# Regrouping the columns of wqkv: matmuls of 512, 512, 384 and 320 columns in place of four of 432

## The chip, the core and the metric

The kernel runs on one core of a Trainium2 chip. The core has a matmul engine (TensorE, called PE in the profile; its weight loads stand in a row of their own, PEld), three engines for elementwise work (VectorE = DVE, ScalarE = ACT, GpSimd = POOL), and a sync engine (SP) that here issues nearly all DMA transfers. The metric is the device time of one execution in microseconds (us), as the median of several runs. Before the change it is 1163.93 us (three runs, 1163.89 to 1163.94).

## The reference

The input x has 2048 rows of D = 576. After a layernorm without scale or shift, two branches run on the same rows and are added to x:

```python
xn = layernorm(x)
return x + A(xn, wqkv, wo) + B(xn, w1, b1, w2, b2)

# A: attention, 32 heads of 18 columns, each row looks at 8 rows: itself and every second row back
q, k, v = split(xn @ wqkv)              # wqkv: 576 x 1728
logits = (q . k[pos - 2*w], w = 0..7) * 18**-0.5     # masked where pos - 2*w < 0
o = softmax(logits) . v[pos - 2*w]
A = o @ wo                              # wo: 576 x 576
# B: feed-forward with a squared relu
B = relu(xn @ w1 + b1)**2 @ w2 + b2     # w1: 576 x 4608, w2: 4608 x 576
```

Everything is float32 in and out. The matmuls get that accuracy by splitting each factor into a high part, rounded to the matmul's own format (F32R), and the low rest; a product is then hi·hi + hi·lo + lo·hi.

## The kernel before

**Blocks.** The 2048 rows are handled in NB = 4 blocks of TB = 512 rows. In every block the feed-forward loop runs over NF = 36 slices of 128 hidden columns: `ffn1` makes one slice of the hidden layer (14 matmuls of 512 columns, line 476), `ffn2` multiplies it with w2 into five PSUM accumulators (14 matmuls of 512 columns, line 499) two slices later. The contraction of 576 is cut into NC = 5 chunks of 128; the fifth holds the last 64 rows twice, so that a high and a low part share one matmul. That is why a full product takes 14 matmuls and not 15.

**Attention.** The 32 heads are dealt into G = 4 groups of 8, CG = 144 columns each. For one group g of one block, `qkv` runs 4 row tiles j of 128 rows; `qkv_rows` issues 14 matmuls (`three`, line 356) in which the rows' transposed x is the stationary operand, loaded as 128 x 128 weights, and the group's columns of wqkv stream past. Those columns are the group's 144 of Q, 144 of K and 144 of V, so each of these matmuls is 432 wide. The result lies in one PSUM tile `wk`, of which there are three, shared with `ffn1`. `qkv_out` copies it out in three ACT instructions: Q into `qo[b]` at the group's own columns, K and V into the group's `kv` tiles. `qkv_close` writes K and V to scratch in DRAM and reads them back with the 14 rows ahead of each partition's rows. Then `attention(b, g)`, a generator, is worked off in pieces on DVE and ACT between the feed-forward steps; it reads its group's columns of `qo[b]` and in the end writes the attention output over them. `o_chunk` and `o_acc` multiply the finished rows with wo into the same five accumulators.

**Weights.** `load_wq(g)` loads the group's columns chunk by chunk (75 DMAs of 128 x 432 into the two `wqr` buffers, line 344), and `split` makes the high part on ACT (line 116) and the low part on DVE (line 118) in the tiles `wqh` and `wql`, of which there is one each, WQ = 448 columns wide. It is called three or four steps ahead of the group's matmuls.

**The order.** `step(n)` goes through the 144 slices of all blocks. The table `pre` says at which step loads and groups stand: in block 0 the groups 1, 2 and 3 start at steps 9, 15 and 20, in later blocks group 0 starts two steps ahead of the block and groups 1 to 3 at its steps 4, 11 and 18. A scheduler then orders the instructions of each engine from a simulation of its own, so the places shift by some instructions; on PE most groups stand as 56 matmuls in a row (4 row tiles x 14), and group 0 of blocks 1 to 3 as 42 and 14 with matmuls of the output product between them.

**The opening.** Block 0's group 0 is written out by hand in `open_rows` (its own order on PE, ACT, DVE and POOL is kept): x is normalized and transposed on PE (line 170), and the 56 matmuls of line 225 follow as their inputs become ready. `load_first` brings the weights for it into one tile `raw`; the high parts are made on ACT, three low parts on DVE and two on POOL (line 200). Two further pieces bear on line numbers below: lines 547 and 549 are the last two output halves, made with matmuls of 256 columns, and line 604 is a warm-up of the matmul engine.

Of the kernel before, what the change touches and what calls it, by code (L numbers as in the profile page):

```python
# [8 lines left out]
F32 = mybir.dt.float32  # L9
F32R = mybir.dt.float32r  # L10
BF16 = mybir.dt.bfloat16
AF = mybir.ActivationFunctionType
# [4 lines left out]
P = 128  # L17
S, D, F = 2048, 576, 4608
H, DH, W, DIL = 32, 18, 8, 2
TB = 512  # L20
NB = S // TB
NJ = TB // P
NC = 5
NF = F // P
G = 4
HG = H // G
CG = HG * DH
HALO = (W - 1) * DIL
# [6 lines left out]
SCALE = DH ** -0.5  # L35
LAG = 2
WARM = 6
WQ, KV = 448, 2688


@with_exitstack
def block_kernel(ctx: ExitStack, tc: tile.TileContext, x, xt, wqkv, wo, w1, b1, w2, b2, out):
    nc = tc.nc
    const = ctx.enter_context(tc.tile_pool(name="const", bufs=1))
    mt = ctx.enter_context(tc.tile_pool(name="mt", bufs=1))
    sb = ctx.enter_context(tc.tile_pool(name="sb", bufs=1))
# [39 lines left out]
    xb, xT, xr, xh, xl, qo, ob, wq = {}, {}, {}, {}, {}, {}, {}, {}  # L86
# [9 lines left out]

    def load_first():
        xb[0] = sb.tile([P, NJ, D], F32, name="xb", bufs=1)
        raw = sb.tile([P, NC, TB], F32, name="xr", bufs=1)[:, :, :3 * CG]
        hi = mt.tile([P, NC, WQ], F32R, name="wqh")[:, :, :3 * CG]  # L100
        lo = mt.tile([P, NC, WQ], F32R, name="wql")[:, :, :3 * CG]
        nc.sync.dma_start(xb[0][:, 0, :288], xv[0, :, 0, :288])
        nc.scalar.dma_start(xb[0][:, 0, 288:], xv[0, :, 0, 288:])
        nc.scalar.dma_start(raw[:, 0], wqkv[0, :, 0])
        nc.sync.dma_start(xb[0][:, 1], xv[0, :, 1])
        for c in range(1, NC):
            nc.sync.dma_start(raw[:, c], wqkv[0, :, c])
        for j in range(2, NJ):
            nc.sync.dma_start(xb[0][:, j], xv[0, :, j])
        for scr in (kscr[0], vscr[0]):  # L110
            nc.sync.dma_start(scr[:PAD], zero)
        return raw, hi, lo
# [16 lines left out]
    def open_x(b):  # L129
        xh[b] = mt.tile([P, NC, TB], F32R, name="xh", bufs=2)  # L130
        xl[b] = mt.tile([P, NC - 1, TB], F32R, name="xl", bufs=2)
# [15 lines left out]
    def row_scale(j):  # L147
        mean_var(0, j)
        rs = sb.tile([P, 1], F32, name="rs", bufs=NJ)
        inverse_std(rs, ln[0, j][:, 1:2])  # L150
        return rs
# [37 lines left out]
    def open_rows():  # L189
        xn = sb.tile([P, NJ, NC * P], F32, name="xt", bufs=1)  # L190
        open_x(0)
        y = open_y()
        raw, hi, lo = first_wq
        rs = {}

        def w_hi(c):
            nc.scalar.activation(hi[:, c], raw[:, c], AF.Copy)

        def w_lo(c, eng):
            eng.tensor_tensor(out=lo[:, c], in0=raw[:, c], in1=hi[:, c].bitcast(F32), op=ALU.subtract)  # L200

        def stats(j, *ks):
            for k in ks:
                bn_stats(0, j, k)

        def scale(j):
            rs[j] = row_scale(j)

        def turn_rows(j):
            turn(y[0 if j % 2 else 3], xn, j, range(NC - 1))  # L210
            turn(y[1 if j % 2 else 4], xn, j, (NC - 1,))

        def take_rows(j, only=None):
            take(y[0 if j % 2 else 3], j, range(NC - 1), only)
            take(y[1 if j % 2 else 4], j, (NC - 1,), only)

        def part(j, i):
            hi, lo = qw[0]
            a, c = divmod(i, 10)
            js = slice(j * P, (j + 1) * P)  # L220
            if (0, j) not in qp:
                qp[0, j] = pw.tile([P, TB], F32, name="wk")
                done[j] = 0
            done[j] += 1
            nc.tensor.matmul(qp[0, j][:, :3 * CG], (xl if a == 1 else xh)[0][:, c, js], (lo if a == 2 else hi)[:, c],  # L225
                             start=done[j] == 1, stop=done[j] == 3 * NC - 1)

        def parts(j, *which):
            for i in which:
                part(j, i)  # L230

        done = {}
        act, dve = nc.scalar, nc.vector
        warm_up(4, TB, xb[0][:, 0, :1])
        stats(0, 0, 1)
        scale(0)
        warm_up(1, TB // 2, rs[0])
        w_hi(0)
        stats(1, 0)
        normalize_rows(xn, 0, rs[0], False, pieces=((0, 2 * P), (2 * P, D)))  # L240
        turn(y[0], xn, 0, (0, 1))
        turn(y[1], xn, 0, (2, 3))
        turn(y[2], xn, 0, (4,))
        w_hi(1)
        stats(1, 1)
        scale(1)
        take(y[0], 0, (0, 1))
        take(y[1], 0, (2, 3))
        normalize_rows(xn, 1, rs[1], False)
        w_hi(2)  # L250
        w_hi(3)
        w_lo(0, dve)
        take(y[2], 0, (4,))
        w_lo(1, nc.gpsimd)
        w_hi(4)
        qkv_open(0, 0, (hi, lo))
        parts(0, 0, 1, 10, 11, 2, 12, 3)
        turn_rows(1)
        take_rows(1, act)
        stats(2, 0, 1)  # L260
        w_lo(2, nc.gpsimd)
        scale(2)
        take_rows(1, dve)
        parts(0, 13, 20, 4)
        parts(1, 0, 1, 2, 3, 20)
        parts(0, 21)
        parts(1, 21, 10, 11, 12, 13, 4)
        nm = minus_mean(2, rs[2])
        normalize_rows(xn, 2, rs[2], True, nm)
        w_lo(3, dve)  # L270
        w_lo(4, dve)
        parts(0, 22)
        parts(1, 22)
        turn_rows(2)
        stats(3, 0, 1)
        scale(3)
        parts(0, 23)
        parts(1, 23)
        parts(0, 24)
        parts(1, 24)  # L280
        take_rows(2)
        nm = minus_mean(3, rs[3])
        qkv_out(0, 0, 0)
        normalize_rows(xn, 3, rs[3], True, nm)
        qkv_out(0, 0, 1)
        parts(2, 0, 1, 2, 3, 20, 21, 22, 23, 10, 11)
        turn_rows(3)
        take_rows(3)
        split_w1(0)
        parts(2, 12, 13, 4, 24)  # L290
        qkv_out(0, 0, 2)
        parts(3, 0, 1, 2, 3, 20, 21, 22, 23, 10, 11, 12, 13, 4, 24)
        split_w1(1)
        last_act = qkv_out(0, 0, 3)
        ffn1(0)
        qkv_close(0, 0)
        return last_act
# [38 lines left out]
    def xsplit(b, c):  # L336
        return xh[b][:, c], xl[b][:, c] if c < NC - 1 else None

    def load_wq(g):
        hi = mt.tile([P, NC, WQ], F32R, name="wqh")[:, :, :3 * CG]  # L340
        lo = mt.tile([P, NC, WQ], F32R, name="wql")[:, :, :3 * CG]
        for c in range(NC):
            r = sb.tile([P, 3 * CG], F32, name="wqr", bufs=2)
            nc.sync.dma_start(r, wqkv[g, :, c])
            split(hi[:, c], lo[:, c], r)
        wq[g] = hi, lo

# [2 lines left out]
    def three(ps, a_hi, a_lo, b_hi, b_lo):  # L350
        mm = []
        for c in range(NC - 1):
            mm += [(a_hi(c), b_hi(c)), (a_hi(c), b_lo(c)), (a_lo(c), b_hi(c))]
        mm += [(a_hi(NC - 1), b_hi(NC - 1)), (a_hi(NC - 1), b_lo(NC - 1))]
        for i, (l, r) in enumerate(mm):
            nc.tensor.matmul(ps, l, r, start=i == 0, stop=i == len(mm) - 1)  # L356

    qw, qp = {}, {}
# [8 lines left out]
    def qkv_rows(b, g, j):  # L367
        hi, lo = qw[g]
        p = qp[g, j] = pw.tile([P, TB], F32, name="wk")
        js = slice(j * P, (j + 1) * P)  # L370
        three(p[:, :3 * CG], lambda c: xh[b][:, c, js], lambda c: xl[b][:, c, js],
              lambda c: hi[:, c], lambda c: lo[:, c])

    def qkv_out(b, g, j):
        p = qp.pop((g, j))
        k, v = kv[g]
        nc.scalar.activation(qo[b][:, j, g * CG:(g + 1) * CG], p[:, :CG], AF.Copy)
        nc.scalar.activation(k[:, HALO + j], p[:, CG:2 * CG], AF.Copy)
        return nc.scalar.activation(v[:, HALO + j], p[:, 2 * CG:3 * CG], AF.Copy)

    def qkv_close(b, g):
        k, v = kv[g]
# [103 lines left out]
    def open_y():  # L486
        return [py.tile([P, TB], F32, name=f"y{i}") for i in range(NC)]
# [136 lines left out]
    pre, mid = {}, {}  # L624

    def at(where, n, f, *a):
        where.setdefault(n, []).append((f, a))
# [7 lines left out]
    for b in range(NB):  # L635
        n0 = b * NF
        if b:
            at(pre, n0 - 26, load_x, b)
            at(pre, n0 - 22, lambda b=b: side.insert(0, layernorm(b)))
            at(pre, n0 - 12, lambda b=b: side.append(normalize(b)))  # L640
            at(pre, n0 - 6, load_wq, 0)
        at(pre, n0 + 13, load_residual, b)
        if b:
            at(pre, n0 - 2, start, b, 0)
        for g, n in ((1, 4), (2, 11), (3, 18)) if b else ((1, 9), (2, 15), (3, 20)):
            at(pre, n0 + n - 3, load_wq, g)
            at(pre, n0 + n, start, b, g)
        for c in range(NC):
            at(pre, n0 + 29 + c, o_weights, c)
            at(mid, n0 + 29 + c, o_chunk, b, c)  # L650
            at(mid, n0 + 31 + 0 + c, o_acc, b, c)
# [68 lines left out]
```

## Time and profile before

| What | us |
|---|---|
| Median of the runs | 1163.93 |
| Profiled execution, its own time | 1163.77 |
| Span of the profiled execution | 1162.1 |
| PE busy in that span | 1157.2 (100%), 5227 matmuls |
| PE weight loads busy | 977.8 (84%) |
| DVE busy | 846.3 (73%) |
| ACT busy | 601.7 (52%) |
| POOL busy | 18.7 (2%) |

The profile is one execution recorded by the hardware. The time of the execution is a little more than its span, which goes from the first instruction to the last. Matmuls are pipelined: one is still in the array when the next begins, so the mean duration of a matmul is longer than the distance from its start to the next start, and that distance is what a matmul costs in a full queue. The chain of work that ended last shows it: it merges matmuls that follow each other without a wait and gives how long each stretch lasted.

### The profile page before, as it was taken

The numbers are of one execution on the slowest core, as the hardware profiler recorded it, in microseconds if no ns is written. First come the engines' busy times: TensorE is split into PE (matmuls) and PEld (weight loads), VectorE is DVE, ScalarE is ACT, GpSimd is POOL, SyncE is SP. The second block draws the span as 40 slices with busy tenths as digits, with TensorE's granted clock in tenths as the row PEclk, the third lists the DMA queues.
The fourth block names the chain that finished last, engine by engine and source line by source line (L and its number), as shares of the span: only waits on it lengthen the run. The fifth ranks groups of instructions, "written<-read, shape, count | busy, mean of one in ns | idle before, by whom it ended". The sixth has DMA issues, their size and how long they took to land.

```text
span 1162.1 us, 14790 instructions
## 1 busy us (share of the span) xinstructions
PE 1157.2 (100%) x5227; PEld 977.8 (84%) x5227; DVE 846.3 (73%) x1370; ACT 601.7 (52%) x1083; POOL 18.7 (2%) x32
## 2 busy tenths in 40 slices
PE   9999999999999999999999999999999999999998
PEld 7888888888888888888888888888888888888887
DVE  6868798892779596985287959698529895857453
ACT  7645445562645454565354545455535455545552
POOL 2000000000000100000000010000000000000000
PEclk9999999999999999999999999999999999999999
DMA  8657436432666556333267554634336735343421
GB/s 281 214 171 242 168 126 226 125 110 68 218 222 208 193 168 207 116 107 117 67 231 232 198 191 154 204 113 128 106 92 227 236 119 190 114 161 114 118 63 51
DMA packets 89386, 185.90 MB, mean 160 GB/s; under 512 B 9952, under 2 KB 37216, under 8 KB 88032
## 3 DMA queue, kind: packets, MB, share of 16 engines
q1 hardware_dynamic: 89024, 184.59, 49.0%
q8 instruction: 41, 0.67, 0.2%
q10 hardware_dynamic: 288, 0.37, 0.1%
q14 instruction: 33, 0.27, 0.1%
HBM read 165.96 MB, written 18.96 MB: 159 GB/s over the span
## 4 chain that ended last, share of the span: by engine, by line
PE 99%; DMA 0%; DVE 0%; POOL 0%; issue 0%; POOLq 0%
PE y L499 44%; PE wk L476 39%; PE wk L356 14%; PE wk L225 1%; PE y L170 0%; DMA xb<-in_x 0%; PE wk L547 0%; DVE st L136 0%; POOL rs L145 0%; DVE xr L549 0%; DVE xt L164 0%; DVE mv L140 0%; DVE rs L144 0%; POOLq L145 0%
## 5 line engine op out<-in xcount | busy, mean ns | idle before, releaser
L499 PE MATMUL y<-hh,w2s 128*128 128x512 f32 x1292 | 319.8, 389 | 0.0
L499 PEld LDWEIGHTS y<-hh,w2s 128*128 128x128 f32 x1292 | 242.5, 188 | 50.3
L476 PE MATMUL wk<-xh,w1h 128*128 128x512 f32 x720 | 210.2, 389 | 0.0
L499 PE MATMUL y<-hl,w2s 128*128 128x512 f32 x718 | 189.5, 389 | 0.0
L476 PE MATMUL wk<-xh,w1l 128*128 128x512 f32 x720 | 186.6, 389 | 0.0
L116 ACT ACTIVATE w1h<-raw 128x640 fp32r<-128x640 f32 x144 | 106.1, 737 | 114.4 <-PE wk L476 112.3
L118 DVE TENSOR_TENSOR w1l<-raw,w1h 128x640 fp32r<-128x640 f32 x144 | 118.0, 819 | 63.8 <-ACT w1h L116 46.0
L122 ACT ACTIVATE w2s<-raw 128x576 fp32r<-128x576 f32 x144 | 97.8, 683 | 119.2 <-PE y L499 117.4
L476 PEld LDWEIGHTS wk<-xh,w1l 128*128 128x128 f32 x720 | 135.2, 188 | 28.1
L499 PEld LDWEIGHTS y<-hl,w2s 128*128 128x128 f32 x718 | 134.8, 188 | 28.0
L476 PEld LDWEIGHTS wk<-xh,w1h 128*128 128x128 f32 x720 | 135.2, 188 | 27.0
L476 PE MATMUL wk<-xl,w1h 128*128 128x512 f32 x576 | 154.0, 389 | 0.0
L124 DVE TENSOR_TENSOR w2s<-raw,w2s 128x512 fp32r<-128x512 f32 (+1 forms) x288 | 118.2, 452 | 45.1 <-ACT w2s L122 43.8
L483 DVE TENSOR_TENSOR hl<-r,hh 128x512 fp32r<-128x512 f32 x144 | 98.9, 687 | 49.4 <-ACT r L482 49.2
L476 PEld LDWEIGHTS wk<-xl,w1h 128*128 128x128 f32 x576 | 108.1, 188 | 22.5
L478 ACT ACTIVATE r<-wk,b1t 128x512 f32<-128x512 f32 x144 | 98.4, 684 | 43.9 <-PE wk L476 43.6
L409 DVE TENSOR_TENSOR pr<-qo,kv 128x1152 f32<-128x1152 f32 x64 | 86.6, 1352 | 37.0 <-DMA kv<-kscr 37.0
L356 PE MATMUL wk<-wqh,xh 128*128 128x432 f32 x300 | 107.4, 358 | 0.0
L356 PE MATMUL wk<-wql,xh 128*128 128x432 f32 x300 | 107.4, 358 | 0.0
L482 ACT ACTIVATE r<-r 128x512 f32<-128x512 f32 x144 | 91.0, 632 | 4.4
L481 ACT ACTIVATE hh<-r 128x512 fp32r<-128x512 f32 x144 | 91.0, 632 | 4.3
L431 DVE TENSOR_TENSOR pr<-lg,kv 128x1152 f32<-128x1152 f32 x64 | 86.8, 1356 | 1.4
(91 smaller groups left out, 961.4 us busy)
## 6 DMA issues: line engine op xcount, KB each, us to landing
raw<-in_w SPq DMA_DIRECT2D x144, 320.0 KB, 3.1
raw<-in_w SPq DMA_DIRECT2D x144, 288.0 KB, 2.8
wqr<-in_wqkv SPq DMA_DIRECT2D x75, 216.0 KB, 3.5
kv<-kscr SPq DMA_DIRECT2D x16, 1008.0 KB, 5.8
kv<-vscr SPq DMA_DIRECT2D x16, 1008.0 KB, 8.4
raw<-in_wo SPq DMA_DIRECT2D x20, 288.0 KB, 2.7
kscr<-kv SPq DMA_DIRECT2D x16, 288.0 KB, 2.7
vscr<-kv SPq DMA_DIRECT2D x16, 288.0 KB, 3.2
```

What stands on the lines that cost most here:

```text
L116: i = nc.scalar.activation(hi, raw, AF.Copy)
L118: i = nc.vector.tensor_tensor(out=lo, in0=raw, in1=hi.bitcast(F32), op=ALU.subtract)
L122: nc.scalar.activation(w[:, :D], raw, AF.Copy)
L124: nc.vector.tensor_tensor(out=w[:, o:o + n], in0=raw[:, a:a + n], in1=w[:, a:a + n].bitcast(F32), op=ALU.subtract)
L356: nc.tensor.matmul(ps, l, r, start=i == 0, stop=i == len(mm) - 1)
L431: nc.vector.tensor_tensor(out=pr.rearrange("p w (a d) -> p w a d", d=DH), in0=at[:, :, :, None].to_broadcast([P, W, HG, DH]), in1=shifted( ...
L476: nc.tensor.matmul(p, l, r, start=i == 0, stop=i == len(mm) - 1)
L478: nc.scalar.activation(r, p, AF.Relu, bias=b1t[:, f:f + 1])
L481: nc.scalar.activation(hh, r, AF.Square)
L482: nc.scalar.activation(r, r, AF.Square)
L483: last_hl[0] = nc.vector.tensor_tensor(out=hl, in0=r, in1=hh.bitcast(F32), op=ALU.subtract)
L499: nc.tensor.matmul(yp[b][c], v, a, start=first and c not in cs[:i], stop=c in last and c not in cs[i + 1:], skip_group_check=True)
```

## The change

The widths of the groups are taken from a table, `WIDE`: 448, 512, 384 and 384 columns in block 0, and 512, 512, 384 and 320 in the other three. Each group still brings its own 144 columns of K and 144 of V, since its attention needs them; the rest of its width is filled with columns of Q in order, whatever group they belong to: 160, 224, 96 and 96 in block 0, 224, 224, 96 and 32 in the others. `QAT` holds where each group's share of Q begins and ends in `qo[b]`. The running totals (160, 384, 480, 576 and 224, 448, 544, 576) are at no group below 144 per group, so a group's Q columns are there when its attention begins. In the matmul's output, K and V now stand first and Q behind them. The host lays wqkv out twice, once for block 0 and once for the others, in rows of 512 columns of which a group uses the first part. The number of matmuls stays the same, and so does the sum of their columns (1728 per row tile and block).

```diff
-WQ, KV = 448, 2688
+WQ, KV = 512, 2688
+WIDE = [(448, 512, 384, 384)] + 3 * [(512, 512, 384, 320)]
+QAT = [[sum(n - 2 * CG for n in w[:g]) for g in range(G + 1)] for w in WIDE]
...
     def load_first():
         xb[0] = sb.tile([P, NJ, D], F32, name="xb", bufs=1)
-        raw = sb.tile([P, NC, TB], F32, name="xr", bufs=1)[:, :, :3 * CG]
-        hi = mt.tile([P, NC, WQ], F32R, name="wqh")[:, :, :3 * CG]
-        lo = mt.tile([P, NC, WQ], F32R, name="wql")[:, :, :3 * CG]
+        raw = sb.tile([P, NC, TB], F32, name="xr", bufs=1)[:, :, :WIDE[0][0]]
+        hi = mt.tile([P, NC, WQ], F32R, name="wqh")[:, :, :WIDE[0][0]]
+        lo = mt.tile([P, NC, WQ], F32R, name="wql")[:, :, :WIDE[0][0]]
...
-            nc.tensor.matmul(qp[0, j][:, :3 * CG], (xl if a == 1 else xh)[0][:, c, js], (lo if a == 2 else hi)[:, c],
+            nc.tensor.matmul(qp[0, j][:, :WIDE[0][0]], (xl if a == 1 else xh)[0][:, c, js], (lo if a == 2 else hi)[:, c],
                              start=done[j] == 1, stop=done[j] == 3 * NC - 1)
...
-    def load_wq(g):
-        hi = mt.tile([P, NC, WQ], F32R, name="wqh")[:, :, :3 * CG]
-        lo = mt.tile([P, NC, WQ], F32R, name="wql")[:, :, :3 * CG]
+    def load_wq(b, g):
+        n = WIDE[b][g]
+        hi = mt.tile([P, NC, WQ], F32R, name="wqh")[:, :, :n]
+        lo = mt.tile([P, NC, WQ], F32R, name="wql")[:, :, :n]
         for c in range(NC):
-            r = sb.tile([P, 3 * CG], F32, name="wqr", bufs=2)
-            nc.sync.dma_start(r, wqkv[g, :, c])
+            r = sb.tile([P, n], F32, name="wqr", bufs=2)
+            nc.sync.dma_start(r, wqkv[min(b, 1), g, :, c, :n])
             split(hi[:, c], lo[:, c], r)
         wq[g] = hi, lo
...
-        three(p[:, :3 * CG], lambda c: xh[b][:, c, js], lambda c: xl[b][:, c, js],
+        three(p[:, :WIDE[b][g]], lambda c: xh[b][:, c, js], lambda c: xl[b][:, c, js],
               lambda c: hi[:, c], lambda c: lo[:, c])
 
     def qkv_out(b, g, j):
         p = qp.pop((g, j))
         k, v = kv[g]
-        nc.scalar.activation(qo[b][:, j, g * CG:(g + 1) * CG], p[:, :CG], AF.Copy)
-        nc.scalar.activation(k[:, HALO + j], p[:, CG:2 * CG], AF.Copy)
-        return nc.scalar.activation(v[:, HALO + j], p[:, 2 * CG:3 * CG], AF.Copy)
+        nc.scalar.activation(qo[b][:, j, QAT[b][g]:QAT[b][g + 1]], p[:, 2 * CG:WIDE[b][g]], AF.Copy)
+        nc.scalar.activation(k[:, HALO + j], p[:, :CG], AF.Copy)
+        return nc.scalar.activation(v[:, HALO + j], p[:, CG:2 * CG], AF.Copy)
...
-    wqkv = rows(A_wqkv).reshape(NC, P, 3, G, CG).transpose(3, 1, 0, 2, 4).reshape(G, P, NC, 3 * CG)
+    q, k, v = rows(A_wqkv).reshape(NC, P, 3, D).transpose(2, 1, 0, 3)
+    wqkv = np.zeros((2, G, P, NC, WQ), k.dtype)
+    for i in range(2):
+        for g in range(G):
+            own = slice(g * CG, (g + 1) * CG)
+            wqkv[i, g, :, :, :WIDE[i][g]] = np.concatenate(
+                [k[:, :, own], v[:, :, own], q[:, :, QAT[i][g]:QAT[i][g + 1]]], 2)
```

More of the change, by code (lines that the diff above doesn't have):

```diff
@@ L98, in load_first @@
         xb[0] = sb.tile([P, NJ, D], F32, name="xb", bufs=1)
-        raw = sb.tile([P, NC, TB], F32, name="xr", bufs=1)[:, :, :3 * CG]
-        hi = mt.tile([P, NC, WQ], F32R, name="wqh")[:, :, :3 * CG]
-        lo = mt.tile([P, NC, WQ], F32R, name="wql")[:, :, :3 * CG]
+        raw = sb.tile([P, NC, TB], F32, name="xr", bufs=1)[:, :, :WIDE[0][0]]
+        hi = mt.tile([P, NC, WQ], F32R, name="wqh")[:, :, :WIDE[0][0]]
+        lo = mt.tile([P, NC, WQ], F32R, name="wql")[:, :, :WIDE[0][0]]
         nc.sync.dma_start(xb[0][:, 0, :288], xv[0, :, 0, :288])
         nc.scalar.dma_start(xb[0][:, 0, 288:], xv[0, :, 0, 288:])
-        nc.scalar.dma_start(raw[:, 0], wqkv[0, :, 0])
+        nc.scalar.dma_start(raw[:, 0], wqkv[0, 0, :, 0, :WIDE[0][0]])
         nc.sync.dma_start(xb[0][:, 1], xv[0, :, 1])
         for c in range(1, NC):
-            nc.sync.dma_start(raw[:, c], wqkv[0, :, c])
+            nc.sync.dma_start(raw[:, c], wqkv[0, 0, :, c, :WIDE[0][0]])
         for j in range(2, NJ):
@@ L640, in block_kernel @@
             at(pre, n0 - 12, lambda b=b: side.append(normalize(b)))
-            at(pre, n0 - 6, load_wq, 0)
+            at(pre, n0 - 6, load_wq, b, 0)
         at(pre, n0 + 13, load_residual, b)
@@ L645, in block_kernel @@
         for g, n in ((1, 4), (2, 11), (3, 18)) if b else ((1, 9), (2, 15), (3, 20)):
-            at(pre, n0 + n - 3, load_wq, g)
+            at(pre, n0 + n - 3, load_wq, b, g)
             at(pre, n0 + n, start, b, g)
```

## The prediction

> **What bounds the kernel now.** I read the page first: span, busy shares, granted clock, and the chain of work that ended last.
>
> ```profile
> span 1162.1 us, 14790 instructions
> PE 1157.2 (100%) x5227; PEld 977.8 (84%) x5227; DVE 846.3 (73%) x1370; ACT 601.7 (52%) x1083; POOL 18.7 (2%) x32
> ...
> PEclk9999999999999999999999999999999999999999
> ...
> PE y L499 44%; PE wk L476 39%; PE wk L356 14%; PE wk L225 1%; PE y L170 0%; DMA xb<-in_x 0%; PE wk L547 0%; DVE st L136 0%; POOL rs L145 0%; DVE xr L549 0%; DVE xt L164 0%; DVE mv L140 0%; DVE rs L144 0%; POOLq L145 0%
> ```
>
> The chain is matmuls from end to end, at full clock, and the lines that change, 356 and 225, hold 15% of it. A busy PE is not proof that it never waits, so the next view was the waits of PE. Its only row is before the real work, in the warm-up:
>
> ```profile
> PE wk L604 <- DVE warm L597: 1.2, 1, 1.2
> ```
>
> After the opening the time is therefore the sum of what each matmul costs in a full queue. That cost is in the chain in order of time, where stretches without a wait stand as one row (start, length, line, count):
>
> ```profile
> 68.48 3.17 PE y L499 x14
> 71.65 10.97 PE wk L356 x56
> 82.62 3.17 PE wk L476 x14
> ...
> 266.39 6.35 PE y L499 x28
> 272.74 8.22 PE wk L356 x42
> 280.96 7.29 PE y L499 x32
> 288.25 2.75 PE wk L356 x14
> 291.00 6.39 PE wk L476 x28
> ...
> 1012.21 10.97 PE wk L356 x56
> ...
> 1157.13 1.44 PE wk L547 x12
> ```
>
> A matmul of 512 columns costs 6.35 / 28 = 226.7 ns, one of 256 columns (line 547) 1.44 / 12 = 120.0 ns, one of 432 columns 10.97 / 56 = 195.9 ns. A straight line through 256 and 512 has a slope of 106.7 / 256 = 0.4167 ns per column and an offset of 13.3 ns; at 432 columns it gives 193.3. So the 432-wide matmul costs 2.6 ns more than its neighbours on both sides lead one to expect. The durations show the same (minimum, median, maximum of one):
>
> ```profile
> L476 PE MATMUL wk<-xh,w1h x720: 387/389/397, 20.7 to 1145.4; 128*128 128x512 f32 x180
> L356 PE MATMUL wk<-wqh,xh x300: 352/358/365, 71.5 to 1022.6; 128*128 128x432 f32 x150
> L547 PEld LDWEIGHTS wk<-hh,w2s x8: 188/192/192, 1156.7 to 1158.0; 128*128 128x128 f32 x8
> L547 PE MATMUL wk<-hh,w2s x8: 278/283/283, 1157.0 to 1158.2; 128*128 128x256 f32 x8
> ```
>
> At 512 the median is 389 and nearly everything lies on it, at 256 the median is the maximum; at 432 the durations are spread over 13 ns, so the stream stutters. The reader is to see also that the stutter outlasts the group. Group 0 of blocks 1 to 3 is cut after 42 matmuls, and the 512-wide ones behind it take 7.29 for 32, where 32 x 226.7 = 7.25; behind the 14 it is 6.39 for 28 in place of 6.35. Behind a full 56 the next 14 take the usual 3.17.
>
> **The change part by part.** *Matmuls.* The count stays, 14 per row tile; only widths move. By the line, 384 columns cost 173.3 ns, 320 cost 146.7, 448 cost 200.0. Nothing in the trace runs at these widths, so the unknown term is the stutter, bounded below by 0 (256 and 512 have none) and above by the 2.6 ns of 432. I take 0, because all new widths are multiples of 64 like 256 and 512, and 432 is not; the upper end is kept for the range.
>
> Block 0, groups 1 to 3: now three rows of 10.97 = 32.91; then 56 x (226.7 + 173.3 + 173.3) = 32.11: -0.80 us. Blocks 1 to 3, each: now 8.22 + 2.75 + 3 x 10.97 = 43.88; then 56 x (226.7 + 226.7 + 173.3 + 146.7) = 43.31: -0.57 us. The stutter behind the 42 and the 14 goes too, 0.04 + 0.04, as group 0 then is 512 wide: -0.65 per block, -1.95 for three.
>
> *Opening.* Group 0 of block 0 grows from 432 to 448 columns.
>
> ```profile
> 7.11 1.76 PE wk L225 x7
> ...
> 9.47 3.55 PE wk L225 x17
> ...
> 13.71 2.80 PE wk L225 x14
> ...
> 17.26 3.60 PE wk L225 x18
> ```
>
> ```profile
> PEld y L170 <- ACT xt L162: 0.6, 2, 0.3
> PEld wk L225 <- ACT xh L116: 0.6, 3, 0.3
> ...
> PEld y L170 <- DVE xt L164: 0.5, 2, 0.3
> ...
> PEld wk L225 <- DVE xl L118: 0.3, 1, 0.3
> ...
> L200 POOL TENSOR_TENSOR wql<-xr,wqh 128x432 fp32r<-128x432 f32 x2 | 2.2, 1117 | 0.0
> ```
>
> The four stretches hold 56 matmuls in 11.71 us, of which 56 x 195.9 = 10.97 is matmul work. 16 more columns each make 56 x (200.0 - 195.9) = +0.23. If the waits for normalized rows (the four rows above, 2.0 us together, none of them for the weights) swallow it all, it is 0. If the longer splits come on the path as well, the two on POOL cost 1117 x 16 / 432 = 41 ns more each and the others less, ten in all: +0.4 at most on top of it. I take +0.23, since most of these matmuls stand behind another matmul.
>
> *What feeds and empties them.* The 75 splits and loads keep their number and sum, but change size, 512 columns being 19% more than 432. They run far ahead: the last split of wqkv begins at 984.9, the last group at 1012.21 in the chain above.
>
> ```profile
> L118 DVE TENSOR_TENSOR wql<-wqr,wqh x75: 595/603/610, 24.4 to 984.9; 128x432 fp32r<-128x432 f32 x75
> ...
> wqr<-in_wqkv SPq DMA_DIRECT2D x75, 216.0 KB, 3.5
> ...
> L377 ACT ACTIVATE qo<-wk 128x144 f32<-128x144 f32 x64 | 18.3, 286 | 96.9 <-PE wk L356 96.1 <-PE wk L225 0.7
> L378 ACT ACTIVATE kv<-wk 128x144 f32<-128x144 f32 x64 | 18.2, 284 | 0.0
> L379 ACT ACTIVATE kv<-wk 128x144 f32<-128x144 f32 x64 | 18.1, 293 | 0.0
> ```
>
> A load lands in 3.5 us, and there it would have to be some 27 us late to be felt; I cost loads and splits at nothing outside the opening. On SP's queue the number of issues is unchanged. A row tile is copied out in 286 + 284 + 293 = 863 ns, and ACT waits for PE there (96.1 us). The narrowest tile, 14 x 146.7 = 2.05 us, still covers that, with three PSUM tiles in turn. The order of engines is nearly as before; near the block borders two of a group's matmuls now stand among the feed-forward's, which costs nothing on a full queue.
>
> *The cover for all this* is that DVE's results stay ahead of PE. The tightest place I found after the opening is in block 2 (start, length):
>
> ```profile
> 703.93 0.82 DVE L118 TENSOR_TENSOR w1l<-raw,w1h 128x640 fp32r<-128x640 f32 x1
> ...
> 707.88 1.29 PE L476 MATMUL wk<-xh,w1l 128*128 128x512 f32 x5
> ```
>
> The low part of w1 is done 3.1 us ahead of its first use. Groups 0 and 1 get 56 x 30.8 ns = 1.72 us longer each, group 2 1.26 shorter, group 3 2.76 shorter: PE is up to 3.4 us later inside a block, which lengthens the lead at this place (behind group 1), and 0.6 earlier behind group 3. At worst attention work displaced by 2.2 us meets a PE that is 0.6 earlier, 2.8 in all, less than the tightest 3.1.
>
> Sum: -0.80 - 1.95 + 0.23 = -2.52 against the profiled execution's 1163.77, so 1161.25; the median of the runs is 0.16 above that execution, which makes 1161.4, or 0.22% less. What a measurement of this kernel can tell from no change is taken as 0.2%, here 2.3 us, so the forecast sits just past that mark.
>
> **The rivals.** *Every width but 256 and 512 pays something.* A smooth curve through the three points puts an excess of 2.6 x (W - 256)(512 - W) / (176 x 80) on the line: 2.2 ns at 448 and 320, 3.0 at 384. That is 224 x 2.2 + 280 x 3.0 = 1.3 us given back: 1162.7. For it: three points cannot tell a curve from a step. Against it: the spread of durations at 432 looks like a stream out of step, not like a fixed price.
>
> *Only odd multiples of 64 stutter.* If the step is 128 columns, 448 and 320 (56 + 168 = 224 matmuls) are off it as 432 is: up to 224 x 2.6 = 0.6 us given back, 1162.0. For it: both clean widths in the trace are multiples of 128.
>
> *The change does nothing.* If a matmul costs a constant plus its columns, the same number of matmuls with the same sum of columns costs the same, and 1163.9 stays. The three rows speak against it: a line through 256 and 432 (0.431 ns per column) would put 512 at 230.4, not 226.7. The Trainium skill, page "TensorE: Matmul & The Clock Gate", section "Back-to-back issue gap", has such a rule for a single stream at full clock: columns / 2.4 plus 2.5 ns. By that rule a set of four groups costs 730 ns before and after, and the time would not move; the trace has 226.7, 195.9 and 120.0 where the rule gives 215.8, 182.5 and 109.2, so it is short by 10.9, 13.4 and 10.8, and it is the 13.4 that the change is about.
>
> *Slower: narrow matmuls wait for their weights.* A weight load is busy for 188 ns, and a matmul of 320 or 384 columns is to cost 146.7 or 173.3. Were loads unable to overlap, 168 x 41 + 280 x 15 = 11 us would be added: about 1172.5. It would decide from a floor of 174 ns per load: 168 x 27.3 + 280 x 0.7 = 4.8 us, the way from 1161.4 to slower by 0.2%. Against it stands line 547, 256 columns at 120.0 ns with loads of 188 to 192 beside them.
>
> *A new wait behind a narrow group.* DVE falls behind there; it needs over 4.8 us of stall against the leads above.
>
> **How the numbers follow.** Forecast 0.45 (its own range 1161.0 to 1161.9: the opening at its ends of 0 and +0.6, and 0.1 to 0.2 for rows rounded to 0.01 in fifteen groups); smooth curve 0.25; odd multiples of 64 0.20; nothing 0.03; weight loads 0.04; new wait 0.03. The range takes in the first three with their opening, 1161.0 to 1163.1, and leaves out 0.1 and a little. The forecast is faster by over 0.2% unless the opening takes its upper end, so of its 0.45 about 0.40 count; a small stutter at odd multiples adds 0.02: faster 0.42. Same gets the curve, most of the odd multiples and the rest of the forecast, 0.52; slower 0.06.
>
> **What would show it.** In the chain of the changed kernel the 56 matmuls of a group should last 9.71 us (384), 8.21 (320) and 12.69 (512), with no wait of PE after the opening, and the stretch behind the 42 should be 7.25 for 32. The opening should end 0.2 to 0.3 us later. Rows of 9.87 and 8.34 would be the curve; 9.71 beside 8.36 the step of 128; 10.5 for 320 the weight loads. A row of PE waiting for DVE would be the wait I excluded.

## The result

| | us |
|---|---|
| Before, median of 20 runs | 1163.85 (1163.74 to 1164.00) |
| Changed, median of 20 runs | 1161.86 (1161.72 to 1162.02) |
| Ratio, 95% interval | 0.9983 (0.9976 to 0.9990) |
| Changed, profiled execution | 1161.89, span 1160.2 |

The change makes the kernel 1.99 us faster, 0.17%. That lies inside the range given, and 0.5 us short of the forecast of 1161.4.

The page of the changed kernel: span, busy times, chain by line. The chain is still matmuls from end to end.

```profile
span 1160.2 us, 14780 instructions
PE 1154.8 (100%) x5227; PEld 966.6 (83%) x5227; DVE 846.0 (73%) x1370; ACT 599.4 (52%) x1083; POOL 18.0 (2%) x32
PE y L502 44%; PE wk L479 39%; PE wk L359 14%; PE wk L227 1%; DMA xb<-in_x 0%; PE y L172 0%; PE wk L550 0%; DVE st L138 0%; POOL rs L147 0%; DVE xr L552 0%; DVE xt L166 0%; DVE mv L142 0%; DVE rs L146 0%; POOLq L147 0%
```

Its waits of PE (total us, times, longest) are all in the first 7 us, so no new wait has come in the body.

```profile
PE wk L607 <- DVE warm L600: 1.2, 1, 1.2
PE wk L605 <- POOL rs L147: 0.2, 1, 0.2
PE y L172 <- DVE xt L166: 0.2, 1, 0.2
```

Its chain in order of time (start, length, line, count; line 359 is now the group's matmuls, 227 the opening's, 479 and 502 the feed-forward's), first the opening, then single groups and what follows them:

```profile
7.22 1.79 PE wk L227 x7
...
9.60 3.64 PE wk L227 x17
...
13.92 2.86 PE wk L227 x14
...
17.46 3.67 PE wk L227 x18
21.14 8.40 PE wk L479 x37
...
71.93 12.69 PE wk L359 x56
...
164.21 9.73 PE wk L359 x56
173.94 3.21 PE wk L479 x14
177.15 3.17 PE y L502 x14
...
281.87 7.25 PE y L502 x32
289.13 3.17 PE wk L359 x14
292.30 6.35 PE wk L479 x28
...
439.66 8.21 PE wk L359 x56
447.87 3.20 PE wk L479 x14
```

The 512-wide group (12.69) costs 226.7 ns per matmul, the 320-wide one (8.21) 146.6 and the 384-wide one (9.73) 173.8. The stretches behind the cut group 0 have become 7.25 and 6.35. New is the row behind a 384-wide group: 14 matmuls of 512 columns last 3.21, the next 14 again 3.17, and behind the 320-wide group it is 3.20. The four stretches of the opening sum to 11.96 in place of 11.71, and the feed-forward begins at 21.14 in place of 20.86 (both 0.16 behind the recorded start of its first matmul, which is used below).

It helps to cut both profiled executions into three parts at two starts in the trace, that of the first feed-forward matmul and that of the last matmul: the opening goes from 20.70 to 20.98 us (+0.28), the body from 1137.59 to 1135.24 (-2.35), the end from 3.78 to 3.96 (+0.18). So the body gives less than the 2.75 forecast for it, and 0.18 is lost at a place that the prediction did not look at.

### The profile page after: what moved, and what is told of

It reads as the page before. It is cut to its first block, busy times and chain, and to the rows that moved or that the text cites. A ratio compares the mean times of both kernels' runs of the same rounds, so it can differ in the third digit from the quotient of the medians.

```text
span 1160.2 us, 14780 instructions
## 1 busy us (share of the span) xinstructions
PE 1154.8 (100%) x5227; PEld 966.6 (83%) x5227; DVE 846.0 (73%) x1370; ACT 599.4 (52%) x1083; POOL 18.0 (2%) x32
## 4 chain that ended last, share of the span: by engine, by line
PE 99%; DMA 0%; DVE 0%; POOL 0%; issue 0%; POOLq 0%
PE y L502 44%; PE wk L479 39%; PE wk L359 14%; PE wk L227 1%; DMA xb<-in_x 0%; PE y L172 0%; PE wk L550 0%; DVE st L138 0%; POOL rs L147 0%; DVE xr L552 0%; DVE xt L166 0%; DVE mv L142 0%; DVE rs L146 0%; POOLq L147 0%
## 5 line engine op out<-in xcount | busy, mean ns | idle before, releaser
L359 PE MATMUL wk<-wqh,xh 128*128 128x512 f32 (+2 forms) x300 | 106.3, 355 | 0.0
L359 PE MATMUL wk<-wql,xh 128*128 128x512 f32 (+2 forms) x300 | 106.3, 355 | 0.0
L118 ACT ACTIVATE wqh<-wqr 128x512 fp32r<-128x512 f32 (+2 forms) x75 | 40.6, 561 | 102.3 <-DMA wqr<-in_wqkv 72.9
```

Source lines behind the costliest of these rows:

```text
L118: i = nc.scalar.activation(hi, raw, AF.Copy)
```

## The experiments

All times are medians; the kernel before, run beside each set, was at 1163.80 to 1163.82. The interval of each ratio is some 0.0009 to either side, 1 us, but medians of ten or more runs of one kernel repeat within about 0.05 us, and the three parts of the trace repeat better still in the body. Comparisons of 0.2 us below rest on medians and traces that agree. The theory: the widths alone move the time, by what a matmul costs at each width. The rivals: the new layout of the data does part of it, and the gain depends on another step than the widths.

### All groups back to 432 wide

```diff
-WIDE = [(448, 512, 384, 384)] + 3 * [(512, 512, 384, 320)]
+WIDE = [(432, 432, 432, 432)] * 4
```

> All groups 432 wide again, with the rest of the change kept: rows of 512 columns in wqh, wql and in DRAM, K and V ahead of Q. Theory (the widths alone move the time): the time of the kernel before, 1163.85 within 0.2, and a group of 56 lasts 10.97 us. Rival (the layout does part of it, for instance by where a chunk begins in memory): a time between 1161.9 and 1163.5, with a group of 56 shorter than 10.97 us.

Measured: 1164.04, ratio 1.0003 (0.9994 to 1.0012). The body lasts 1137.59 as before, to the hundredth, although a chunk of weights now begins every 512 columns: with the widths as they were, another place of the columns in SBUF leaves the cost of the matmuls as it was. But the kernel is 0.2 slower, and in the trace all of that is behind the last matmul (3.98 in place of 3.78). The layout does have a part, then, and it is a loss.

### Block 0 alone, and the later blocks alone

```diff
+WIDE = [(448, 512, 384, 384)] + 3 * [(432, 432, 432, 432)]    # block 0 alone
+WIDE = [(432, 432, 432, 432)] + 3 * [(512, 512, 384, 320)]    # later blocks alone
```

> Block 0 as in the change (448, 512, 384, 384), the other blocks 432. From the trace of the changed kernel: groups 1 to 3 of block 0 should last 12.69 + 9.73 + 9.73 us and give 0.75 us, less 2 x 0.04 behind the two 384-wide groups, and the opening should cost 0.2: 0.4 to 0.6 us faster than before, about 1163.4. Rival (the opening's cost is not real and the changed kernel only began late): 0.7 faster, 1163.15.

> Block 0 all 432, blocks 1 to 3 as in the change. From the trace of the changed kernel each of these blocks gives 0.57 + 0.08 less 0.067 for entering and leaving the 384-wide group and 0.02 for the 320-wide one: 0.55 to 0.6 per block, 1.65 to 1.75 in all, about 1162.15. If block 0 is worth more than its opening costs, this is slower than the whole change; rival (the opening takes all that block 0 gives): equal to the whole change, 1161.9.

Measured, block 0 alone first: 1163.57, ratio 0.9998 (0.9989 to 1.0007), and 1162.36, ratio 0.9988 (0.9980 to 0.9997). Both are 0.2 above the expected time, which is the loss at the end that both carry (3.98 us in both traces). Against the kernel with all groups at 432 they are 0.47 and 1.68 faster, inside what was expected, and 0.47 + 1.68 = 2.15 is the whole change's 1164.04 - 1161.86 = 2.18. The parts add up, so no coupling of the blocks is seen. Block 0's own parts are unequal: its body is 0.64 shorter than with 432, of which the median keeps 0.47, so the opening at 448 columns costs some 0.17.

### What a matmul costs at 20 widths

```diff
+WIDE = [(448, 512, 384, 384), (496, 464, 480, 288), (480, 432, 416, 400), (448, 440, 424, 416)]
...
+WIDE = [(448, 512, 384, 384), (512, 488, 428, 300), (492, 484, 352, 400), (504, 452, 468, 304)]
...
-            nc.sync.dma_start(r, wqkv[min(b, 1), g, :, c, :n])
+            nc.sync.dma_start(r, wqkv[b, g, :, c, :n])
```

> Twelve widths in blocks 1 to 3: 496, 464, 480, 288; 480, 432, 416, 400; 448, 440, 424, 416. Read for each: the mean distance of two starts within the group against the line (columns + 32) / 2.4. Theory A (a stutter wherever the matmul's own time comes near the 188 ns that a weight load is busy): excess over the line at 400 to 464, most between 416 and 448, fading to 0 at 496, none at 288. Theory B (a stutter at every width that is no multiple of 128, 320 being an exception): excess at all of them, 288 included. Theory C (multiples of 32 run better than multiples of 16): 416, 448 and 480 lower than 400, 424, 432, 440, 464 and 496.

> Twelve more widths, to find the edges of the band: 512, 488, 428, 300; 492, 484, 352, 400; 504, 452, 468, 304. Theory A (the stutter belongs to a band that begins where the matmul's own time passes the 188 ns of a weight load, between 424 and 432 columns, and ends between 480 and 496): 488, 492, 504 and 352 on the line (columns + 32) / 2.4 within 0.3 ns; 452, 468 and 484 2 to 4 ns above it; 428 (191.7 ns by the line) 0 to 2 above. Theory B (divisibility): 428, 300, 492, 484, 452, 468 and 488 (no multiples of 16) above the line by at least the 2.5 ns of 432. Widths of 300 and 304 should lie 1 to 2 ns under the line, as 288 does.

The 24 groups of the two sets hold 21 widths, as 480, 416 and 400 stand twice; 512 is the 21st. The host lays wqkv out four times here, once for each block. A group of 288 columns holds no Q, so its copy of Q is left out.

The chain in order of time, of the first set and of the second. The rows are groups in the order of `WIDE` above, some left out; a count of 42 or 55 is a group that is cut.

```profile
272.25 9.24 PE wk L359 x42
328.09 11.49 PE wk L359 x55
384.03 12.13 PE wk L359 x56
440.59 7.37 PE wk L359 x56
...
614.50 10.97 PE wk L359 x56
669.90 10.45 PE wk L359 x56
724.78 10.08 PE wk L359 x56
845.97 8.51 PE wk L359 x42
900.66 11.20 PE wk L359 x56
956.32 10.64 PE wk L359 x56
```

```profile
328.47 12.10 PE wk L359 x55
385.03 10.98 PE wk L359 x56
440.46 7.65 PE wk L359 x56
559.18 9.24 PE wk L359 x42
615.02 12.03 PE wk L359 x55
671.48 9.02 PE wk L359 x56
...
846.13 9.52 PE wk L359 x42
...
902.17 11.57 PE wk L359 x56
958.21 11.84 PE wk L359 x56
1014.53 7.72 PE wk L359 x56
```

The two kernels took 1162.63 and 1163.04 us, in one run each. Length over count, against the line (columns + 32) / 2.4 that 256 and 512 lie on:

| Columns | ns each | over the line |
|---|---|---|
| 288, 300, 304 | 131.6, 136.6, 137.9 | -1.7, -1.7, -2.1 |
| 352 | 161.1 | +1.1 |
| 400, 416, 424 | 180.0, 186.6, 190.0 | 0.0, -0.1, 0.0 |
| 428, 432, 440 | 196.1, 195.9, 200.0 | +4.4, +2.6, +3.3 |
| 448, 452, 464 | 202.6, 206.6, 208.9 | +2.6, +4.9, +2.2 |
| 468, 480, 484 | 211.4, 216.6, 218.7 | +3.1, +3.3, +3.7 |
| 488, 492, 496 | 220.0, 220.0, 220.0 | +3.3, +1.7, 0.0 |
| 504 | 226.7 | +3.3 |

Theory B (divisibility by 128) falls: 400, 416 and 424 are on the line. Theory C falls too: 480, a multiple of 32, pays more than 464, a multiple of 16, and 424 is neither and pays nothing. Theory A comes nearest, with a band that begins not at 400, as first expected, but between 424 and 428, where the line passes 190 to 192 ns, and reaches up to 492. But it does not end cleanly, as 504 costs what 512 costs and 488 and 492 what 496 costs, which the expectation had on the line; and 352 pays 1.1 outside the band. Nor is the price a matter of how evenly the starts follow each other: at 488, which pays 3.3, all 55 distances of two starts are 220 ns, while at 416 they change between 184 and 190 and at 424 between 187 and 193, and both pay nothing. What is shown is the table, for groups between matmuls of 512 columns; a rule that gives all of it was not found. For the change it says that 384 and 320 are clean, and that 448 is not: its 2.6 ns is that of 432.

### The tiles' stride in SBUF, the layout in DRAM, the order of Q, K and V

Three kernels on the 0.2 us at the end. The first is the kernel before with wider tiles, the second the kernel before with the larger input, the third has all groups at 432 and K and V ahead of Q, with the input at its old size.

```diff
-WQ, KV = 448, 2688
+WQ, KV = 512, 2688                       # first
...
+    wqkv = np.stack([np.pad(wqkv, ((0, 0), (0, 0), (0, 0), (0, 512 - 3 * CG)))] * 2)   # second
...
-    wqkv = np.zeros((2, G, P, NC, WQ), k.dtype)
+    wqkv = np.zeros((1, G, P, NC, 3 * CG), k.dtype)      # third
```

> The kernel before with one number changed: the rows of wqh and wql are 512 columns wide in SBUF in place of 448, of which 432 are used. It asks where the 0.2 us come from that the kernel with all groups at 432 is slower than before, all of it behind the last matmul. Theory (the larger tiles move the other tiles' addresses, the output's among them, and the last stores land later): 0.2 slower than before, 1164.0, with 3.97 us from the start of the last matmul to the end of the span. Rival (the new layout of wqkv in DRAM or the order of K, V and Q does it): as before, 1163.8 and 3.78 us.

> The kernel before with one thing changed: wqkv lies in DRAM as in the change, in rows of 512 columns and twice, with the old order of Q, K, V and 432 columns used. It asks for the 0.2 us behind the last matmul that all kernels with the changed layout show. Theory (the larger input moves what lies behind it in DRAM, the output too, and the last stores complete later): 1164.0, 3.97 us from the start of the last matmul to the end. Rival (the order of the columns): 1163.82 and 3.78 us.

> All groups 432 wide, K and V ahead of Q as in the change, rows of 512 columns in SBUF, but wqkv in DRAM once and in rows of 432, so that it has the size it had before. Theory (DRAM): 1163.82 and 3.78 us from the start of the last matmul to the end. Rival (order of the columns): 1164.0 and 3.97 us.

Measured: 1163.85 (ratio 1.0002, 0.9993 to 1.0010), 1164.06 (1.0001, 0.9993 to 1.0010) and 1163.85 (1.0000, 0.9991 to 1.0009), with 3.78, 3.99 and 3.78 us behind the last matmul's start. My theory of the tiles' addresses fell; the larger input in DRAM alone brings the 0.2. The sync engine's last waits for the output's stores (total, times, longest) show where it is, in the kernel before, in the second and in the third:

```profile
SPq L715 <- DMA out<-xr: 1.6, 3, 0.8
```

```profile
SPq L716 <- DMA out<-xr: 1.8, 3, 1.2
```

```profile
SPq L724 <- DMA out<-xr: 1.6, 3, 0.8
```

The last stores are waited for 0.2 us longer, though their number and size are the same and, in all three traces, the last two are issued 0.10 and 0.77 us after the last matmul's start. A larger input may move what lies behind it in DRAM, the output too; no run shows that it is this which matters.

### Half the weights

```diff
+        hs = slice(j * P, j * P + 64)
+        for _ in range(3):
+            three(p[:64, :WIDE[b][g]], lambda c: xh[b][:, c, hs], lambda c: xl[b][:, c, hs],
+                  lambda c: hi[:, c], lambda c: lo[:, c])
         three(p[:, :WIDE[b][g]], lambda c: xh[b][:, c, js], lambda c: xl[b][:, c, js],
```

> In blocks 1 to 3 each row tile first runs its 14 matmuls three times over with only 64 columns of weights in place of 128 (42 added matmuls, whose result the full 14 then overwrite). Widths 432, 448, 480, 368; 512, 496, 288, 432; 512, 512, 304, 400. The time, some 350 us longer, does not matter; the distance of two starts among the 42 does. Theory A (the band belongs to the time of the weight load): with loads half as long the offset of 13.3 ns shrinks or the band moves down, so that 432, 448 and 480 come to lie evenly on one line. Rival (the band belongs to the width of the moving rows): 432 at 195.8, 448 at 202.7, 480 at 216.7 again, uneven in the same rhythm.

The edit is in the helper that all groups but the opening's use, so it reaches block 0 too. A row of the durations (minimum, median, maximum), and the table by stretch, each holding the first 42 matmuls of a group with 64 columns of weights (window, length, PE busy and count, PEld busy and count, clock, DMA); the widths are 512, 384, 432, 448 and 480 in this order:

```profile
L359 PEld LDWEIGHTS wk<-wqh,xh x1200: 133/135/193, 71.6 to 1511.5; 128*64 128x64 f32 x129, 128*128 128x128 f32 x43
```

```profile
71.81:81.47 9.66, 9.66 (x42) 5.69 (x42) 1.00 0.90 268
161.22:168.50 7.28, 7.28 (x42) 5.69 (x42) 1.00 0.18 52
369.23:377.28 8.05, 8.05 (x42) 5.69 (x42) 1.00 0.22 68
455.92:464.42 8.50, 8.50 (x42) 5.67 (x42) 1.00 0.72 228
545.95:555.17 9.23, 9.23 (x42) 5.76 (x42) 1.00 0.35 101
```

The kernel took 1653.56 us in one run, 490 us more than before and not some 350, which does not bear on the distances. A load of 64 columns lasts 135 ns in place of 188. The Trainium skill, page "TensorE: Matmul & The Clock Gate", section "LDWEIGHTS (loading the stationary operand)", gives columns / 1.2, by which half the columns take an estimated 53 ns less; the difference agrees. The whole duration does not: by the same formula an estimate for 128 columns is 107 ns, and 188 were measured. The matmuls cost 230.0 (512), 173.3 (384), 191.7 (432), 202.4 (448) and 219.8 ns (480). Neither side holds. Theory A expected less offset or an even line, and 512 now pays 3.3 ns that it did not pay before, 480 pays 6.4. The rival expected the same costs as with full loads, and 432 now lies 1.6 under the line. So the width of the moving rows alone does not set the extra cost. Whether it is the load, or the 64 output rows in place of 128 that come with it, this run cannot tell. What ran ahead counts too: 42 such matmuls of 432 columns cost 191.7 ns each behind matmuls of 512 columns (three times), and 191.1 or 195.6 behind a row tile of their own group. The 14 matmuls of 448 columns with full weights that follow 42 with half of them cost 206.5 here, where the first set of widths gave 202.6. One width can have more than one rhythm, then, and what makes it stays open.

### Widths chosen from the table

```diff
+WIDE = [(432, 512, 496, 288)] + 3 * [(512, 512, 416, 288)]
...
+WIDE = [(448, 496, 496, 288)] + 3 * [(512, 512, 416, 288)]
```

> Widths chosen from the measured ones that lie on the line or under it and pay little where the width changes: 432, 512, 496, 288 in block 0 and 512, 512, 416, 288 in the others. Against the changed kernel: each later block saves the 0.067 and 0.020 of the 384- and 320-wide groups and has 0.05 less for 288, together 0.13, so 0.40; block 0 saves 0.28 in the opening and pays 0.19 in its three groups. Theory: 0.5 us faster than the changed kernel, 1161.4. Rival (prices at a change of width depend on the neighbours and do not carry over, or the opening's 0.28 is spread of the first transfer): 1161.6 to 1161.9.

> As the kernel with chosen widths, but block 0 with 448, 496, 496, 288. The three later groups of block 0 last 56 x (220.0 + 220.0 + 131.6) in place of 56 x (226.7 + 220.0 + 131.6), 0.37 less; the opening at 448 costs 0.2 to 0.3 more. Theory: 1161.35, 0.1 faster than with 432 in the opening. Rival (the opening costs more than it gives): 1161.5 to 1161.6.

Measured: 1161.45, ratio 0.9979 (0.9970 to 0.9988), and 1161.22, ratio 0.9978 (0.9969 to 0.9987), against the changed kernel's 1161.86. The prices at a change of width carried over: the body is 1135.04 and 1134.66, where 1135.24 less 0.40 and plus 0.19 gives 1135.03, and 0.37 less than that 1134.66. The second came out 0.13 below its expectation: with a body 0.38 shorter it is 0.23 faster, so 448 columns in the opening cost 0.15 and not 0.2 to 0.3.

### The same without padding in DRAM

```diff
-    wqkv = np.zeros((2, G, P, NC, WQ), k.dtype)
+    wqkv = np.zeros((2, NC, P, 3 * D), k.dtype)
...
-            nc.sync.dma_start(r, wqkv[min(b, 1), g, :, c, :n])
+            nc.sync.dma_start(r, wqkv[min(b, 1), c, :, sum(WIDE[b][:g]):sum(WIDE[b][:g + 1])])
```

> The kernel of e11 with wqkv in DRAM in two copies of 1728 columns without the padding to 512 per group: 8.8 MB in place of 10.5, 4.4 before the change. Theory (where the output lies decides, not the padding or the number of copies as such): the 0.2 us may go or stay; if the start of the last matmul stands 3.78 us before the end again, the time is 1161.0, if 3.97, 1161.2. Rival (more bytes of input alone lengthen the end): 3.97 us, as 8.8 MB is more than 4.4.

Measured: 1160.98, ratio 0.9975 (0.9966 to 0.9985), the fastest of all, 0.9 below the changed kernel. The body is the same 1134.66; the end has 3.63 us, less than in the kernel before, and the last waits are shorter:

```profile
SPq L726 <- DMA out<-xr: 1.5, 3, 0.7
```

More bytes of input do not lengthen the end by themselves, so that rival falls; at 4.4, 8.8 and 10.5 MB the end was 3.78, 3.63 and 3.97. Nor is wqkv all that moves it. The two kernels of the 20 widths and the one with half the weights hold the same four padded copies, 21 MB; the first two have an end of 3.96 and 3.95, the third 3.66. What sets the end stays open.

## Why the prediction was right, and where its sizes were off

**The bound** held. PE has no wait in the body, and the body's time is the sum of its matmuls' costs. The leads of DVE, the copies out of PSUM and the loads cost nothing, as worked out.

**The matmuls.** The step "I take 0, because all new widths are multiples of 64" gave the right number for 384 and 320, but by luck: the table shows no such rule, with 424 clean and 448 and 480 not. For 448 the step failed: 202.6 ns and not 200.0. That falls into the opening alone. The prediction also read the excess as a stutter, from durations spread over 13 ns at 432. In its own rows 512 spans 10 ns, and by the distances above 488 pays with an even stream while 416 and 424 pay nothing with an uneven one, so the spread was no evidence against a curve.

**The term that was left out** is the price of a change of width. The prediction saw it where 432 was cut (7.29 for 7.25) and let it vanish with 432, without asking whether the new widths have one. They do: in the changed kernel 0.02 on the way into a 384-wide group (9.73 against 56 x 173.3 = 9.71) and 0.04 on the way out (3.21 against 3.17); for 320 a gain of less than 0.01 on the way in, 0.03 on the way out by the row (0.025 by the starts). Five groups of 384 and three of 320 make 5 x 0.067 + 3 x 0.02 = 0.39 us of the forecast 2.75, which leaves 2.36; the body gave 2.35.

**The opening** was put at +0.23 and came to +0.28 in the profiled pair. The stretches of its matmuls grew by 0.25 (11.71 to 11.96), the transposes between them took 0.07 less, and the first matmul began 0.11 later (7.11 and 7.22). That begin follows the landing of the first rows of x and differs from run to run: it is 7.40 in the first kernel with chosen widths and 7.10 in the second. So one pair of traces is a weak measure, and the medians say less: 0.17 from block 0 alone, 0.15 from the two kernels with chosen widths. At the table's prices 448 for 432 columns would be 56 x 6.7 = 0.38, so by the medians over half of it does not show in the time. That the waits for rows take it up, which the prediction had as its lower end, fits and was not tested.

**The end** was not in the sum at all. The prediction costed the loads of wqkv at nothing, which holds for the loads, and did not ask what a larger input does elsewhere: 0.18 in the trace, 0.2 in the medians.

Together: -2.52 + 0.39 + 0.05 + 0.18 = -1.90, against 1161.89 - 1163.77 = -1.88 between the two profiled executions. In the medians it is -2.52 + 0.39 - 0.07 + 0.2 = -2.00, against -1.99.

That 1161.86 still lies in the forecast's own 1161.0 to 1161.9 is luck: its upper end was slack for a longer opening and for rounded rows, and the two terms that were left out used it up. The forecast of 0.22% lay just past the 0.2% that the prediction takes as its mark, and the 0.17% measured lies short of it.

**The rivals.** The time came out near that of "only odd multiples of 64 stutter" (1162.0), but not by its mechanism: 320 is such a multiple and lies on the line. The smooth curve fell, since 384 would have cost 176.3. That the change does nothing fell, and with it the rule of the Trainium skill, page "TensorE: Matmul & The Clock Gate", section "Back-to-back issue gap", columns / 2.4 plus 2.5 ns, by which the sum would not have moved: a single price per matmul does not describe this stream of loads and matmuls, in which 424 and 428 columns are 6 ns apart. The section itself gives that rule for isolated matmuls and says that in a stream of loads and matmuls both set the distance. The 131 ns that it gives there for 512 columns are not what is measured here either, 226.7. Narrow matmuls did not wait for their weights, and no wait behind the narrow group came up.

## What to carry to other kernels

In a kernel that one engine fills from end to end, read the distance of starts for each shape and compare shapes with each other; a shape that lies off the line of its neighbours is a gain of its own, worth here 2.6 ns in each of 840 matmuls, and it can be found by running many shapes in one kernel. Count also what a change of shape costs at its two edges, since the price at the old edges did not go away with them here. Where the time to be won is 0.2%, cut the span into opening, body and end before judging: the layout of an input, which left the body as it was, took back a tenth of this gain.

## What was not expected of the hardware

Between matmuls of 512 columns, the widths run from 428 to 492 columns with a load of 128 x 128 weights before each cost 1.7 to 4.9 ns more than (columns + 32) / 2.4, 288 to 304 columns 1.7 to 2.1 less, and 504 as much as 512. With 64 columns of weights the same widths pay other amounts, 512 among them, and what ran ahead changes the price at one width (191.1 to 195.6 ns at 432). And a larger input in DRAM, with nothing else of the kernel changed but the places in it that are loaded, lengthened the time behind the last matmul from 3.78 to 3.99 us, with the same stores.
